# Attention and mixture of experts: the transposed maxima of the next pair one score slot earlier

## Chip, cores and metric

The kernel runs on one core of a Trainium2 chip. The metric is device microseconds from start to end of one execution. Shorter is better. The times below are three executions and one profiled execution of the kernel before.

## What is computed

Attention with rotary embedding, and then a top-1 mixture of experts over its result:

```
q, k, v: (4, 8, 576, 64) fp32                # 4 batches, 8 heads, 576 positions
q_rot, k_rot = rotate(q), rotate(k)
scores = q_rot @ k_rot^T / 8
attn = exp(scores - max(scores)); attn /= sum(attn) + 1e-9
x = (attn @ v) laid out as (2304, 512)       # 2304 tokens
logits = normalized x . normalized expert_emb / tau      # 8 experts
out[token] = gate * (relu(x @ w1[expert]) @ w2[expert])  # 512 -> 1024 -> 512
```

The expert of a token is the argmax of its logits, and its gate is that expert's softmax probability. Most matrix products are made of fp16 or bf16 halves (a high part and a rest), so that the result is close to fp32.

## The kernel before

**Pairs and slots.** The 32 heads are worked on as 16 pairs of heads (0 to 15). A pair has nine score slots: four key tiles of 128 for each head and one tile shared by both (slot 4). In the text, S7 of pair 11 is the score product of slot 7 of that pair (smm, L226 and L230), E7 its exponential on ScalarE (sexp, L241), and M3 of pair 13 the product of slot 3 that is made only to find the row maxima (maxmm, L185). VectorE reduces each of these to a column of the tile m9 (maxred, L191).

**Where the maxima go.** When all nine columns of a pair are there, maxend does two things. Step 0 (L198) transposes m9 on TensorE into a PSUM bank, tile mt. Step 1 copies it on ScalarE as shift minus maximum, in fp16, to the tile mr (L202), and two DMAs of SyncE (L203, L204) put it into row 64 of the tile QB, where the score product of L230 adds it to the scores. So a pair's first L230 needs those DMAs.

**The bank.** mt lies in the PSUM bank with the tag bk0. In turn the same bank holds mt, the first five value products of a pair (pv, group 0; the fp32 ones are L260, the fp16 ones L281 to L283) and, in a few places, tiles of the routing (rank, L503 and L504). Whoever writes it next waits for the last reader: for mt that is VectorE's division of the value products of the pair before (pvend, L298 and L299), or its copy of the rank tile (L509, L510). The first L260 of a pair waits for ScalarE's copy of mt (L202). Score tiles S and M share a ring of three PSUM tiles.

**The order.** Nothing is scheduled by hand on the engines. Each step is entered with a time in units of one score slot, the list is sorted, and the steps are issued in that order; each engine then runs its own instructions in that order and waits by semaphores. Pair i starts at g0 = 9 i. The times come from the table TIMES (L38):

```
mev(f"M{s}", m0 + md * s + cfg.get("mmt", .2), maxmm, i, s)      # m0 = g0 - 14
ev(f"W{s}", g0 + PVL + s + cfg.get("pvt", .3) - .81, pvw, i, s)  # PVL = 7.5; puts the L260 into the score product
me = cfg.get("mend", 12)
mev("Z0", g0 - L + me, maxend, i, 0)                             # L = 14
mev("Z1", g0 - L + me + cfg.get("med", .7), maxend, i, 1)        # med = 0.3
```

For pairs 0 and 1 a table of its own takes the place of mend. In the middle of the kernel three pairs are in work at a time: during the slots of pair 11 TensorE makes the scores of pair 11, the value products of pair 10 and then 11, the maxima products of pair 13, and the transposition of the maxima of pair 12.

**Routing and experts.** Beside the last pairs VectorE computes logits, ranks and lists (finish, early), with one exponential on ScalarE (L516). At the end of early, SyncE loads the number of the most used expert from the tile est (L870), and issues its eight weight loads (L872). ScalarE converts the weights (conv, L694, L695, L698) in between the exponentials of pair 15. Then follow 22 tiles of 128 tokens through two layers.

Of the kernel before, what the change touches and what calls it, by code (L numbers as in the profile page):

```python
# [34 lines left out]
SY = SX * SW * SW  # L35

ORDER = ((0, 0, 0), (1, 0, 0), (0, 0, 1), (1, 0, 1), (0, 1, 0), (1, 1, 0))
TIMES = {"pe1": 1.06, "pvlead": 7.5, "mend": 11.5, "fin": 3, "w": 0.3, "pbufs": 13, "vat": -1, "med": 0.3, "sst": 1.6, "mct": 0.25, "pvt": 0.3, "pe0": 0.9, "d": 0.6, "rdt": 0.9, "e": 0.5, "c0": 135, "fin2": 2.5, "sq": 0.8, "max0": [[-21, 0.5], [-5, 1], [4.5, 0.9]], "start": [-30, -13, -4, 2.6], "le": -3.5, "vet": 1.2, "mmt": 0.2, "mlead": 14, "klo": 1, "me0": [-13.5, 6.6], "mdir": 3, "ve0": -16, "v0": 3, "pl": [[0, 0, 0, 0], [0, 3, 2, 5]], "setup": [-59.5, -25, -20.9, -19.2, -59.4, -14], "l3": -12, "rk": 14, "ls": 52, "dt": 0.6, "t0": 148.5, "ta": 0.25, "wlead": 10, "cut1": 126, "glead": 20, "s": 0.6, "fin3": -0.45, "r01": [[-30.0, -29.1, -28.2, -27.3, -24.6, -26.4, -25.5, -23.7, -22.8, -21.0], [-25, -24.9, -24.8, -15.5, -14, -20.8, -20.7, -20.6, -15, -13.5]], "bw": 0, "cp": [0, 2, 4, 6], "c0d": 1, "lg1": 0.5, "free": [[2.3, 2.3, 1], [3.5, 3.5, 1], [6.2, 6.2, 0]], "fgap": 1.2}  # L38


def attention(tc, ctx0, ctx, ctx2, ins, xs, R, at, bank, cfg):
# [744 lines left out]
def build(tc, ins, out, cfg=None):  # L786
    cfg = {**TIMES, **(cfg or {})}
    nc = tc.nc
# [217 lines left out]
```

## Times and profile before

| | us |
|---|---|
| three executions | 592.35, 588.22, 587.76 |
| median | 588.22 |
| profiled execution, its own time | 585.0 |
| its span | 582.8 |
| TensorE busy (weight loads apart) | 524.2 |
| VectorE busy | 491.9 |
| ScalarE busy | 344.1 |
| GpSimd busy | 252.1 |

Attention takes about the first 330 us of the span, and the experts the rest. A row of the timeline is the start in us, the duration in us, the engine (PE TensorE's products, PEld its weight loads, DVE VectorE, ACT ScalarE, SPq SyncE's queue), the line, the operation, what it writes and reads, the shapes, how many were merged, and in brackets how long the engine was idle before it and what ended that. Ends of matrix products are modelled.

### The profile page before, as it was taken

What the parts mean: (1) busy time and instruction counts of PE and PEld (TensorE: products, weight loads), DVE (VectorE), ACT (ScalarE), POOL (GpSimd) and SP (SyncE); (2) the same over time, 40 slices, a digit from 0 to 9 for tenths busy, and PEclk for the clock granted to TensorE, in tenths of its full rate; (3) what the DMA queues carried; (4) which work ended last, traced back from release to release, by engine and by line L of the source; (5) the groups of instructions that cost most, each with busy time, mean ns of one, the idle gap of its engine ahead of it and who ended that gap; (6) DMA issues with size and microseconds to landing.
All of it is one profiled execution on the core that took longest, in us unless ns stands there. A gap on an engine that the chain in (4) does not pass through costs nothing. (4 is left out here: it accounts for less than half of the span.)

```text
span 582.8 us, 15753 instructions
## 1 busy us (share of the span) xinstructions
PE 524.2 (90%) x6062; PEld 413.6 (71%) x6062; DVE 491.9 (84%) x778; ACT 344.1 (59%) x578; POOL 252.1 (43%) x174
## 2 busy tenths in 40 slices
PE   1599999999998999799887899999999999999993
PEld 0336778877887887678787888778778768768761
DVE  5886898889899889988865575699999999999981
ACT  2133444555544555246347543679989989989962
POOL 7668765556687555710005132213323323323211
PEclk9999999999999999799997989999999999999998
DMA  8577566568465785145126301378995115431100
GB/s 293 140 199 230 147 184 188 143 183 217 127 186 170 210 214 154 31 111 156 50 84 243 121 4 38 94 234 281 311 326 174 49 47 179 134 112 39 57 21 32
DMA packets 42945, 86.11 MB, mean 148 GB/s; under 512 B 8422, under 2 KB 25702, under 8 KB 42864
## 3 DMA queue, kind: packets, MB, share of 16 engines
q1 hardware_dynamic: 39344, 74.46, 42.3%
q0 software_dynamic: 3520, 10.58, 5.7%
q8 instruction: 49, 0.80, 0.6%
q14 instruction: 32, 0.26, 0.2%
HBM read 115.84 MB, written 10.56 MB: 217 GB/s over the span
## 5 line engine op out<-in xcount | busy, mean ns | idle before, releaser
L699 DVE SCALAR_TENSOR_TENSOR w<-raw,w 128x1024 f16<-128x1024 f32 x148 | 177.3, 1239 | 11.4 <-ACT w L698 11.1
L241 ACT ACTIVATE p<-st 128x576 f32<-128x576 f32 x144 | 93.7, 650 | 134.6 <-PE st L230 131.8
L698 ACT ACTIVATE w<-raw 128x1024 f16<-128x1024 f32 x148 | 148.5, 1057 | 0.0
L191 DVE TENSOR_REDUCE m<-mx 128x1 f32<-128x576 f32 x144 | 106.0, 749 | 33.2 <-PE mx L185 21.6
L735 PEld LDWEIGHTS <-w 128*128 128x128 f16 x2112 | 121.3, 99 | 4.7
L735 PE MATMUL h<-xTm,w 128*128 128x128 f16 x2112 | 123.6, 220 | 0.0
L756 PE MATMUL yp<-w,hT 128*128 128x512 f16 x528 | 120.8, 379 | 0.0
L260 PEld LDWEIGHTS pv<-V,p 128*128 128x128 f32 (+1 forms) x640 | 87.4, 188 | 24.3 <-issue 13.8
L761 POOL DMA_INDIRECT out<-y,sidx x22 | 32.8, 1490 | 159.6 <-ACT y L760 159.6
L226 PE MATMUL st<-QAB,KA 128*128 128x288 f16 x320 | 90.0, 302 | 12.5 <-DVE m L191 11.5
L260 PE MATMUL pv<-V,p 128*128 128x73 f32 (+1 forms) x640 | 94.6, 261 | 4.7 <-ACT mr L202 4.7
L250 DVE TENSOR_TENSOR p<-p 128x576 f16<-128x576 f32 x80 | 92.5, 1159 | 0.6 <-ACT p L241 0.6
L756 PEld LDWEIGHTS <-hT 128*128 128x128 f16 x528 | 50.8, 98 | 52.9 <-issue 0.2
L230 PE MATMUL st<-QAB,KB 65*128 65x288 f16 x320 | 70.2, 302 | 0.2 <-DMA QAB<-mr 0.2
L282 PE MATMUL pv<-V,p 128*128 128x72 f16 (+1 forms) x480 | 63.8, 203 | 0.0
L281 PE MATMUL pv<-V,p 128*128 128x73 f16 (+1 forms) x480 | 63.4, 201 | 0.0
L283 PE MATMUL pv<-V,p 128*128 128x73 f16 (+1 forms) x480 | 63.2, 199 | 0.0
L185 PE MATMUL mx<-KA,QAB 128*128 128x288 f16 x260 | 52.1, 290 | 0.8 <-ACT p L241 0.8
L281 PEld LDWEIGHTS <-p 128*128 128x128 bf16 (+1 forms) x480 | 48.7, 106 | 4.4 <-issue 1.4
L282 PEld LDWEIGHTS <-p 128*128 128x128 bf16 (+1 forms) x480 | 47.1, 103 | 2.5
L283 PEld LDWEIGHTS <-p 128*128 128x128 f16 (+1 forms) x480 | 47.9, 105 | 0.0
L149 POOL TENSOR_TENSOR qlo<-q,qhi 128x576 f16<-128x576 f32 x14 | 19.0, 1358 | 64.6 <-ACT qhi L144 64.6
(159 smaller groups left out, 703.7 us busy)
## 6 DMA issues: line engine op xcount, KB each, us to landing
raw<-w SPq DMA_DIRECT2D x152, 512.0 KB
q<-qk SPq DMA_DIRECT2D x16, 576.0 KB
k<-qk SPq DMA_DIRECT2D x16, 576.0 KB
vt<-vt SPq DMA_DIRECT2D x16, 320.0 KB
v<-v SPq DMA_DIRECT2D x16, 320.0 KB
QAB<-qhi SPq DMA_DIRECT2D x32, 144.0 KB
KA<-khi SPq DMA_DIRECT2D x64, 72.0 KB
xs<-x SPq DMA_DIRECT2D x8, 512.0 KB
```

Of the source, the lines that this page charges most:

```text
L191: nc.vector.tensor_reduce(out=st[i]["m9"][:, s:s + 1], in_=st.pop(("mx", i, s))[:, :, :288], op=ALU.max, axis=AX.XY)
L226: nc.tensor.matmul(ps[:, c, :288], lhsT=KA[n][:, cols(s, h)], rhs=QA[n][:, H0[h] + c * 288:H0[h] + c * 288 + 288], start=(h == hs[0]), sto ...
L241: nc.scalar.activation(out=p.rearrange("p (c x) -> p c x", c=2), in_=st.pop(("s", i, s))[:, :, :288], func=AF.Exp, scale=0.125)
L250: nc.vector.tensor_tensor(out=lo, in0=p, in1=hi, op=ALU.subtract)
L260: nc.tensor.matmul(o, lhsT=lt, rhs=rt, start=first, stop=False, skip_group_check=True)
L281: nc.tensor.matmul(o[:, 0:73], lhsT=ph, rhs=vv[:, 0:73], start=False, stop=False, skip_group_check=True)
L282: nc.tensor.matmul(o[:, 1:73], lhsT=ph, rhs=vv[:, 73:145], start=False, stop=False, skip_group_check=True)
L283: nc.tensor.matmul(o[:, 0:73], lhsT=pl, rhs=vv[:, 0:73], start=False, stop=(kk == 4), skip_group_check=True)
L698: nc.scalar.activation(out=d[:, 0], in_=raw[c], func=AF.Copy, scale=SW)
L699: nc.vector.scalar_tensor_tensor(out=d[:, 1], in0=raw[c], scalar=SW, in1=d[:, 0], op0=ALU.mult, op1=ALU.subtract)
L735: nc.tensor.matmul(ps[:, f], lhsT=wd[:, wi, jj * 512 + f * 128:jj * 512 + f * 128 + 128], rhs=xt[:, xi, 2 * jp + jj], start=(jp == 0 and k ...
L756: nc.tensor.matmul(ps, lhsT=ht[:, hi, 2 * c + ii], rhs=wd[:, wi, ii * 512:(ii + 1) * 512], start=(c == 0 and k == 0), stop=(c == 3 and k = ...
```

## The change

One number of the table is changed, mend:

```diff
-TIMES = {"pe1": 1.06, "pvlead": 7.5, "mend": 11.5, "fin": 3, ...
+TIMES = {"pe1": 1.06, "pvlead": 7.5, "mend": 10.5, "fin": 3, ...
```

The transposition of pair i moves from g0 - 2.5 to g0 - 3.5 and the copy from g0 - 2.2 to g0 - 3.2, for pairs 2 to 15. That is from slot 6 of the pair before to its slot 5. The DMAs go with the copy. On SyncE the order stays as it was, and so do VectorE's and GpSimd's orders. Three places show what moves (the number at the end of a name is that of the tile; tiles made later have other numbers where the order changed).

TensorE, in the slots of pair 11, the transposition of the maxima of pair 12 (m_12; mx_1 is M1 of pair 13, pv with p_7 is pair 10's):

```order
 L185 LDWEIGHTS QAB_132
 L185 MATMUL mx_1_3636<-KA_133,QAB_132 128x288
+L198 MATMUL mt_3648<-ident,m_12_3287 9x128
 L281 LDWEIGHTS p_7_3371
 L281 MATMUL pv_3544<-V_0_141,p_7_3371 128x73
```

It now stands behind M1, ahead of nine value products and S6; it stood behind M2, ahead of nine value products and S7.

ScalarE, the same slots: the exponential of the routing (L516) and the exponentials E5, E6, E7 of pair 11 (p_5, p_6, p_7):

```order
 L241 ACTIVATE p_4_3587<-st_4_3576 128x576
 L241 ACTIVATE p_5_3634<-st_5_3627 128x576
+L202 ACTIVATE mr_3660<-mt_3648,shiftt 9x128
 L516 ACTIVATE dd_3487<-dd_3487 128x80
-L241 ACTIVATE p_6_3671<-st_6_3664 128x576
-L202 ACTIVATE mr_3690<-mt_3679,shiftt 9x128
+L241 ACTIVATE p_6_3677<-st_6_3670 128x576
 L241 ACTIVATE p_7_3704<-st_7_3697 128x576
```

The copy stood behind L516 and E6 and now stands ahead of both.

ScalarE, in the slots of pair 14, the copy of the maxima of pair 15, the last one ahead of the weight loads on SyncE:

```order
 L241 ACTIVATE p_5_4550<-st_5_4541 128x576
-L241 ACTIVATE p_6_4571<-st_6_4564 128x576
-L202 ACTIVATE mr_4587<-mt_4576,shiftt 9x128
+L202 ACTIVATE mr_4566<-mt_4552,shiftt 9x128
+L241 ACTIVATE p_6_4577<-st_6_4570 128x576
 L241 ACTIVATE p_7_4611<-st_7_4604 128x576
```

It stood behind E6 and now stands behind E5.

## Rows read from the trace of the kernel before

**Rows 1.** View of the tile mr: who waited for it (us, times).
```profile
  PEld pv L260: 10.4, 15
  PE pv L260: 4.7, 8
```
**Rows 2.** Timeline (columns as said above), maxima of pair 5, old place.
```profile
119.06 0.34 ACT L202 ACTIVATE mr<-mt,shiftt 9x128 f16<-9x128 f32 x1
...
119.36 0.28 PE L226 MATMUL st<-QAB,KA 128*128 128x288 f16 x1 [0.23 <-DVE m L191]
...
119.49 0.41 PE L260 MATMUL pv<-V,p 128*128 128x73 f32 x2
```
**Rows 3.** Timelines of VectorE and TensorE, maxima of pair 5, new place.
```profile
114.59 0.19 DVE L299 TENSOR_TENSOR xe<-pv,pvr 128x40 f32<-128x40 f32 x1
...
116.18 0.20 PE L281 MATMUL pv<-V,p 128*128 128x73 f16 x1
...
117.47 0.28 PE L226 MATMUL st<-QAB,KA 128*128 128x288 f16 x1 [0.81 <-DVE m L191]
```
**Rows 4.** Timeline, maxima of pair 2.
```profile
69.02 0.44 PE L260 MATMUL pv<-V,p 128*128 128x73 f32 x2 [0.20 <-ACT mr L202]
...
70.29 0.76 DVE L191 TENSOR_REDUCE m<-mx 128x1 f32<-128x576 f32 x1 [0.40 <-PE mx L185]
```
**Rows 5.** Timeline, maxima of pair 12, from the new place to S7.
```profile
239.86 0.27 PE L281 MATMUL pv<-V,p 128*128 128x73 f16 x1
...
240.95 0.15 DVE L510 COPY cnt<-rank 128x8 f32<-128x8 f32 x1
...
241.75 1.14 DVE L250 TENSOR_TENSOR p<-p 128x576 f16<-128x576 f32 x1
...
242.52 0.42 PE L198 MATMUL mt<-ident,m 128*9 128x128 f32 x1
243.18 0.28 PE L226 MATMUL st<-QAB,KA 128*128 128x288 f16 x1
```
**Rows 6.** Timeline, maxima of pair 12, S7 of pair 11 and what follows.
```profile
245.35 0.44 PE L260 MATMUL pv<-V,p 128*128 128x73 f32 x2 [1.89 <-ACT mr L202]
...
246.64 0.76 DVE L191 TENSOR_REDUCE m<-mx 128x1 f32<-128x576 f32 x1 [1.26 <-PE mx L185]
```
**Rows 7.** Windows: span, length, busy us of PE, PEld, DVE, ACT, POOL, granted clock, DMA.
```profile
238.00:242.00 4.00, 4.00 (x27) 3.49 (x27) 4.00 (x8) 0.65 (x1) 3.92 (x3) 0.50 0.00 0
246.00:250.00 4.00, 4.00 (x30) 3.43 (x28) 2.87 (x10) 2.60 (x5) 0.00 (x0) 0.57 0.19 42
```
**Rows 8.** Timeline, maxima of pair 13, S7 of pair 12 and what follows.
```profile
263.47 0.28 PE L226 MATMUL st<-QAB,KA 128*128 128x288 f16 x1
...
264.43 0.44 PE L260 MATMUL pv<-V,p 128*128 128x73 f32 x2 [0.68 <-ACT mr L202]
...
265.70 0.76 DVE L191 TENSOR_REDUCE m<-mx 128x1 f32<-128x576 f32 x1 [1.68 <-PE mx L185]
```
**Rows 9.** Timeline, maxima of pair 14, S7 of pair 13 and what follows.
```profile
281.83 0.28 PE L226 MATMUL st<-QAB,KA 128*128 128x288 f16 x1
...
282.97 0.44 PE L260 MATMUL pv<-V,p 128*128 128x73 f32 x2 [0.85 <-ACT mr L202]
...
284.24 0.76 DVE L191 TENSOR_REDUCE m<-mx 128x1 f32<-128x576 f32 x1 [1.22 <-PE mx L185]
```
**Rows 10.** Timelines of ScalarE and VectorE, from the maxima of pair 15 to the weights.
```profile
296.37 0.65 ACT L241 ACTIVATE p<-st 128x576 f32<-128x576 f32 x1 [0.56 <-PE st L230]
...
298.00 0.14 DVE L588 CAST est<-em 1x1 int32<-1x1 f32 x1
...
298.07 0.34 ACT L202 ACTIVATE mr<-mt,shiftt 9x128 f16<-9x128 f32 x1
...
305.31 1.06 ACT L694 ACTIVATE ws<-raw 128x1024 f32<-128x1024 f32 x1 [3.85 <-issue]
```
**Rows 11.** View of line L870, SyncE: duration in ns, first and last start.
```profile
L870 SPq TENSOR_LOAD <-est x1: 802/802/802, 299.9 to 299.9; - x1
```

More of the change, by code (lines that the diff above doesn't have):

```diff
@@ L37 @@
 ORDER = ((0, 0, 0), (1, 0, 0), (0, 0, 1), (1, 0, 1), (0, 1, 0), (1, 1, 0))
-TIMES = {"pe1": 1.06, "pvlead": 7.5, "mend": 11.5, "fin": 3, "w": 0.3, "pbufs": 13, "vat": -1, "med": 0.3, "sst": 1.6, "mct": 0.25, "pvt": 0.3, "pe0": 0.9, "d": 0.6, "rdt": 0.9, "e": 0.5, "c0": 135, "fin2": 2.5, "sq": 0.8, "max0": [[-21, 0.5], [-5, 1], [4.5, 0.9]], "start": [-30, -13, -4, 2.6], "le": -3.5, "vet": 1.2, "mmt": 0.2, "mlead": 14, "klo": 1, "me0": [-13.5, 6.6], "mdir": 3, "ve0": -16, "v0": 3, "pl": [[0, 0, 0, 0], [0, 3, 2, 5]], "setup": [-59.5, -25, -20.9, -19.2, -59.4, -14], "l3": -12, "rk": 14, "ls": 52, "dt": 0.6, "t0": 148.5, "ta": 0.25, "wlead": 10, "cut1": 126, "glead": 20, "s": 0.6, "fin3": -0.45, "r01": [[-30.0, -29.1, -28.2, -27.3, -24.6, -26.4, -25.5, -23.7, -22.8, -21.0], [-25, -24.9, -24.8, -15.5, -14, -20.8, -20.7, -20.6, -15, -13.5]], "bw": 0, "cp": [0, 2, 4, 6], "c0d": 1, "lg1": 0.5, "free": [[2.3, 2.3, 1], [3.5, 3.5, 1], [6.2, 6.2, 0]], "fgap": 1.2}
+TIMES = {"pe1": 1.06, "pvlead": 7.5, "mend": 10.5, "fin": 3, "w": 0.3, "pbufs": 13, "vat": -1, "med": 0.3, "sst": 1.6, "mct": 0.25, "pvt": 0.3, "pe0": 0.9, "d": 0.6, "rdt": 0.9, "e": 0.5, "c0": 135, "fin2": 2.5, "sq": 0.8, "max0": [[-21, 0.5], [-5, 1], [4.5, 0.9]], "start": [-30, -13, -4, 2.6], "le": -3.5, "vet": 1.2, "mmt": 0.2, "mlead": 14, "klo": 1, "me0": [-13.5, 6.6], "mdir": 3, "ve0": -16, "v0": 3, "pl": [[0, 0, 0, 0], [0, 3, 2, 5]], "setup": [-59.5, -25, -20.9, -19.2, -59.4, -14], "l3": -12, "rk": 14, "ls": 52, "dt": 0.6, "t0": 148.5, "ta": 0.25, "wlead": 10, "cut1": 126, "glead": 20, "s": 0.6, "fin3": -0.45, "r01": [[-30.0, -29.1, -28.2, -27.3, -24.6, -26.4, -25.5, -23.7, -22.8, -21.0], [-25, -24.9, -24.8, -15.5, -14, -20.8, -20.7, -20.6, -15, -13.5]], "bw": 0, "cp": [0, 2, 4, 6], "c0d": 1, "lg1": 0.5, "free": [[2.3, 2.3, 1], [3.5, 3.5, 1], [6.2, 6.2, 0]], "fgap": 1.2}
 def attention(tc, ctx0, ctx, ctx2, ins, xs, R, at, bank, cfg):
```

## The prediction

> **What bounds the kernel now.** I first asked who waits for the copy that is moved: the weight loads ahead of L260 wait 10.4 us for it in 15 places, and the products themselves stand idle for 4.7 us in 8 [rows 1]. The reader should see that these two differ: most of the 15 waits cost TensorE nothing, because something else held it at the same moment. So I went through the places in the timeline, one by one, and asked at each what would be late next.
>
> In the even middle of the attention (maxima of pairs 3 to 11) the old place looks like that of pair 5 [rows 2]. S7 begins at 119.36, released by VectorE's reduction, and L260 follows 0.13 us later, as it does where nothing is waited for. The copy ended at 119.40, in time by a hair. VectorE sets the pace there; the wait for the copy runs beside the wait for the reduction.
>
> In the last four places the picture is another. At the maxima of pair 12 TensorE is idle for 1.89 us ahead of L260, and VectorE then stands idle for 1.26 us waiting for the maxima product that comes after it [rows 6]. At pair 13 it is 0.68 us and then 1.68 us of VectorE's [rows 8], at pair 14 0.85 and 1.22 us [rows 9]. There the copy is late because ScalarE does squares, the routing's exponential and E6 first, and TensorE holds up everybody. The chain goes S7, maxima product, reduction. At pair 15 the copy matters through SyncE: it ends at 298.41, its two DMAs are ahead of the load of est in SyncE's order, and that load starts only at 299.9 [rows 11] although est was written at 298.14. The weight loads follow, and ScalarE stands for 3.85 us before its first conversion at 305.31 [rows 10].
>
> **The change part by part.** Nothing is added or removed; 14 transpositions, copies and pairs of DMAs move one slot forward.
>
> *Transposition, pairs 2 to 11.* At the new place of pair 5 TensorE is there at 116.18. The bank was given back at 114.78 (L299), 1.40 us earlier, and S6 waits 0.81 us for VectorE anyway [rows 3]. The transposition lengthens the queue by less than that, so it costs nothing; if that cover were gone, it would cost its own time, which leaves the old place. For pairs 3 to 11 I count 0. Bounds: 0.1 us lost over the nine, and 1.0 us won if ScalarE's squares in two of them hold more than they seem to.
>
> *Maxima of pair 2.* TensorE waits 0.20 us for the copy, and VectorE 0.40 us for TensorE after it [rows 4]. I take 0.3 us, between 0.20 and 0.40.
>
> *Maxima of pair 12.* Here the bank is not free at the new place: the rank tile of the routing lies in it. TensorE is there at 239.86, but VectorE reads the rank tile until 241.10 [rows 5]. So the transposition, and behind it nine value products, S6, M2 and S7, wait until 241.16, if I allow the 0.05 us that lie between a reduction's end and its follower elsewhere (an estimate): a new stall of 1.30 us. The work from 239.86 to the start of S7 at 243.18 is 3.32 us, the transposition included, and 0.13 us more bring L260: 241.16 + 3.32 + 0.13 = 244.61, against 245.35. The copy is done long before, as it no longer stands behind L516 and E6. Gain 0.74 us, and VectorE's idle 1.26 us has room for it.
> The clock adds to it. TensorE was granted half rate (1.2 GHz) at the stall, 0.50 in 238 to 242, and again 0.57 in 246 to 250, after its idle 1.89 us [rows 7]. If the second stretch goes with that idle time, up to 4.0 x (1 - 0.57) = 1.72 us come on top: 2.46 us. If instead half rate lasts through S7, the 1.29 us from L260 to the reduction after it [rows 6] take up to as much again, and the gain is 0.74 - 1.29 = -0.5 us. I take 1.0 us, near the value at unchanged rates; bounds -0.5 and 2.4.
> The Trainium skill (TensorE: Matmul & The Clock Gate, A second HAM failure mode: psum-queue depth-cycling) says that short idles between groups of products, while the engine goes round its PSUM banks, are enough to throw the clock back and forth. That speaks against this change, which puts a wait for a bank in a stretch at half rate; by it the lower bound would hold here and the sum would be 2.7 us. The trace agrees so far that 1.89 us of idle stood ahead of the second stretch.
>
> *Maxima of pair 13.* L260 would follow S7's start by 0.13 us, at 263.60 instead of 264.43: 0.83 us [rows 8]. The transposition's time moves from ahead of S7 to ahead of S6, which cancels. Bounds 0.68 (idle alone) and 0.9.
>
> *Maxima of pair 14.* The same: 281.96 instead of 282.97, 1.01 us [rows 9]. The rank tile of this pair is read earlier, so I count no stall. Bounds 0.85 and 1.2 (VectorE's idle).
>
> *Maxima of pair 15.* The copy stands behind E5 instead of E6, so it can start when E5 ends at 297.02 at the latest, instead of 298.07 [rows 10]. SyncE comes to est 1.05 us earlier, at 298.85, still later than est is written. I take 1.05 us: ScalarE's wait for the weights is the longest of this stretch and TensorE runs dry behind it. Bounds 0, if the weights come no earlier, and 1.2.
>
> No queue is passed that would lose by it: SyncE's order is the same, and of GpSimd nothing moves. VectorE's order is the same too.
>
> Sum: 0 + 0.3 + 1.0 + 0.83 + 1.01 + 1.05 = 4.2 us. The experts start from the lists and the weights that the attention's end and SyncE give them, so they move forward as they are. The profiled execution took 585.0 us (span 582.8 and 2.2 us around it), which gives 580.8. The median of the runs shown is 588.2, 3.2 us above; on that footing I predict **584.0 us**.
>
> **The rivals.**
> *Nothing arrives.* The gains of pairs 12 to 14 fall where VectorE is as full as TensorE (4.00 of 4.00 us in 238 to 242 [rows 7]), and the weights' landing is set by something else. For it: the nine even pairs show that shape. Against it: VectorE's idle times behind each wait. 588.2 us, within half a microsecond.
> *Half rate goes on* through S7 after the new stall, the lower bound of that place: pair 12 gives -0.5 instead of 1.0, 2.7 us in all, 585.5 us. For it: the new stall lies at half rate. Against it: the longer idle goes.
> *More than forecast.* The nine even pairs have room of their own and S7 starts 0.3 us earlier in each: 2.7 us more, 581.3 us. Against it: 119.36 is VectorE's release.
> *Slower: the transposition waits for more of VectorE's queue than it needs.* If its wait counts every instruction issued before it, not just L299, then at pair 5 it waits for the reduction that releases S7 at 119.36 [rows 2]. S6 would come no earlier than 119.3 instead of 117.47, at least 1.8 us in each of nine pairs, some 16 us: 600 us with the gains taken off. It decides from a wait beyond the 1.3 us that S6 leaves. Against it: at pair 12 the old transposition started at 242.52 while a subtraction issued before it ran from 241.75 to 242.89 [rows 5]. That the change does nothing is excluded by the order.
>
> **How the numbers follow.** Forecast 0.60, nothing arrives 0.19, half rate 0.11, more than forecast 0.05, slower 0.05. The forecast's own bounds are the sums of the lower ends, 0.2 - 0.1 - 0.5 + 0.68 + 0.85 + 0 = 1.1 us, and of the upper ends, 0.4 + 1.0 + 2.4 + 0.9 + 1.2 + 1.2 = 7.1 us: 581.1 to 587.1. The range takes in the case of nothing too: **581.0 to 588.4**. One per cent, about what a measurement can tell from no change, is 5.9 us: faster than 582.3 needs the upper quarter of the forecast's bounds or the case of more, 0.15 + 0.05 = 0.20. Slower by over 1% is the slower rival, 0.05. Within 1%: 0.75.
>
> **What the profile after would show.** L260 no longer waits for L202 anywhere from pair 2 on. At the new place of pair 12 the transposition starts 0.06 us after L510, behind some 1.3 us of idle, and at no other pair does TensorE wait there. The reductions after S7 of pairs 12 and 13 lose about 0.8 and 1.0 us of idle. L870 starts some 0.7 us after est is written, instead of 1.8. Between the copy of pair 3 and that of pair 11 the distance stays as it was. Wrong would be a stall at L198 in the even pairs, or an L694 that comes as late as before, relative to E5 of pair 14.

## The result and the profile after

The changed kernel takes **583.8 us** in the median of 14 executions (580.4 to 586.5), the kernel before 589.4 us beside it (14 executions, 584.2 to 593.9). The ratio is 0.9908, with a 95% interval of 0.9879 to 0.9936: 5.4 us less, between 3.8 and 7.1. The profiled execution took 584.7 us, with a span of 582.5 us, all but the 582.8 us of before. The two profiles can therefore be compared place by place, but not by their spans.

The view of the tile mr in the kernel after answers to [rows 1]. What is left is pair 1, which was not moved:

```profile
  PEld pv L260: 0.7, 1
  PE pv L260: 0.2, 1
```

The view of TensorE's waits from 40 to 305 us (engine, line, waited for: us in total, times, longest) shows one wait at the transposition L198, and one alone:

```profile
PE st L226 <- DVE m L191: 12.8, 27, 1.2
PE rank L503 <- DVE xe L299: 2.4, 1, 2.4
PE rank L503 <- DVE ohall L495: 1.5, 1, 1.5
PE mt L198 <- DVE nrm L511: 1.3, 1, 1.3
```

In the even middle the timeline shows the transposition of pair 5 with no wait ahead of it, and S6 released by VectorE's reduction as it was in [rows 3]:

```profile
118.46 0.41 PE L185 MATMUL mx<-KA,QAB 128*128 128x288 f16 x2
118.71 0.27 PE L198 MATMUL mt<-ident,m 128*9 128x128 f32 x1
...
120.00 0.28 PE L226 MATMUL st<-QAB,KA 128*128 128x288 f16 x1 [0.71 <-DVE m L191]
```

At pair 12 the new wait stands in TensorE's timeline, and VectorE's and ScalarE's timelines show what ends it and what follows. They answer to [rows 5, 6]:

```profile
243.44 0.37 PE L198 MATMUL mt<-ident,m 128*9 128x128 f32 x1 [1.34 <-DVE nrm L511]
```
```profile
241.72 1.35 DVE L506 TENSOR_SCALAR nrm<-nrm 128x10 f32<-128x10 f32 x1
242.99 0.23 DVE L509 TENSOR_TENSOR rk<-rank,ohall 128x80 f32<-128x80 f32 x1
243.14 0.15 DVE L510 COPY cnt<-rank 128x8 f32<-128x8 f32 x1
243.22 0.20 DVE L511 RECIPROCAL nrm<-nrm 128x10 f32<-128x10 f32 x1
...
245.12 1.28 DVE L515 TENSOR_TENSOR dd<-dd,nrm 128x80 f32<-128x80 f32 x1
...
251.02 0.17 DVE L527 TENSOR_SCALAR gt<-gt 128x10 f32<-128x10 f32 x1
```
```profile
243.85 0.36 ACT L202 ACTIVATE mr<-mt,shiftt 9x128 f16<-9x128 f32 x1 [1.54 <-PE mt L198]
246.44 0.27 ACT L516 ACTIVATE dd<-dd 128x80 f32<-128x80 f32 x1 [2.23 <-DVE dd L515]
```

The copy is now 2.6 us ahead of the routing's exponential L516, which itself waits for VectorE's L515. VectorE's reduction after S7 waits 0.11 us where it waited 1.26 [rows 6], but the reduction behind it waits 1.41 us where it waited 0.39. At pair 13 VectorE's reduction after S7 waits 0.64 us where it waited 1.68 [rows 8]. At pair 15 the load of est starts at 299.5, 0.6 us after est is written, and the first conversion waits 3.44 us, not 3.85 [rows 10, 11]. VectorE's timeline, ScalarE's, and the view of L870:

```profile
265.99 0.76 DVE L191 TENSOR_REDUCE m<-mx 128x1 f32<-128x576 f32 x1 [0.64 <-PE mx L185]
```
```profile
297.15 0.65 ACT L241 ACTIVATE p<-st 128x576 f32<-128x576 f32 x1 [0.56 <-PE st L230]
297.70 0.34 ACT L202 ACTIVATE mr<-mt,shiftt 9x128 f16<-9x128 f32 x1
...
304.92 1.06 ACT L694 ACTIVATE ws<-raw 128x1024 f32<-128x1024 f32 x1 [3.44 <-issue]
```
```profile
L870 SPq TENSOR_LOAD <-est x1: 802/802/802, 299.5 to 299.5; - x1
```

**Why the spans are alike.** The first three rows are TensorE's timeline after, in the slots of pair 1; the rest are windows of the same trace (span, length, busy us of PE, PEld, DVE, ACT, POOL, granted clock, DMA). The last three answer to [rows 7].

```profile
63.45 0.44 PE L226 MATMUL st<-QAB,KA 128*128 128x288 f16 x1
...
68.64 0.28 PE L226 MATMUL st<-QAB,KA 128*128 128x288 f16 x1
68.76 0.34 PE L260 MATMUL pv<-V,p 128*128 128x73 f32 x2
```
```profile
60.00:65.00 5.00, 5.00 (x47) 3.65 (x47) 3.35 (x8) 1.47 (x3) 3.45 (x3) 1.00 0.15 34
238.00:242.00 4.00, 3.25 (x39) 2.63 (x38) 3.97 (x7) 0.34 (x1) 3.92 (x3) 0.65 0.10 21
246.00:250.00 4.00, 4.00 (x36) 3.50 (x35) 2.41 (x7) 2.12 (x5) 0.30 (x1) 0.57 0.00 0
280.00:284.00 4.00, 4.00 (x36) 3.41 (x35) 2.13 (x5) 1.85 (x4) 0.00 (x0) 0.57 0.06 10
```

The score product of 288 columns lasts 0.44 us up to 66.9 us and 0.28 us from 68.64 on: half rate (1.2 GHz) and full rate (2.4 GHz). In the trace before it lasts 0.28 to 0.30 us from 62.6 us on. That is 6 us more at half rate. E5 of pair 1 starts at 69.68 us, 3.0 us later than in the trace before, just ahead of the first moved transposition at 69.72; at E0 of pair 2 it is 2.5 us. The window view doesn't tell this, for it gives 1.00: the trace has no clock record ahead of 68.56 us (62.12 in before), and a stretch without a record is shown as 1.00. A further half-rate stretch of 3.4 us stands near 280 us, where before had none. So the profile of after lost about 2.5 us by E0 of pair 2 and some at 280, and won them back in the last pairs.

### The profile page after: what moved, and what is told of

It reads as the page before. It is cut to its first block, busy times and chain, and to the rows that moved or that the text cites. A ratio compares the mean times of both kernels' runs of the same rounds, so it can differ in the third digit from the quotient of the medians.

```text
span 582.5 us, 15755 instructions
## 1 busy us (share of the span) xinstructions
PE 526.4 (90%) x6062; PEld 416.1 (71%) x6062; DVE 491.4 (84%) x778; ACT 344.4 (59%) x578; POOL 248.7 (43%) x174
## 5 line engine op out<-in xcount | busy, mean ns | idle before, releaser
L241 ACT ACTIVATE p<-st 128x576 f32<-128x576 f32 x144 | 93.5, 650 | 136.4 <-PE st L230 132.7
L226 PE MATMUL st<-QAB,KA 128*128 128x288 f16 x320 | 91.2, 306 | 13.7 <-DVE m L191 12.8
L260 PEld LDWEIGHTS pv<-V,p 128*128 128x128 f32 (+1 forms) x640 | 89.2, 191 | 18.9 <-issue 14.3
L260 PE MATMUL pv<-V,p 128*128 128x73 f32 (+1 forms) x640 | 94.7, 261 | 0.2 <-ACT mr L202 0.2
L250 DVE TENSOR_TENSOR p<-p 128x576 f16<-128x576 f32 x80 | 91.4, 1147 | 0.5 <-ACT p L241 0.5
L230 PE MATMUL st<-QAB,KB 65*128 65x288 f16 x320 | 71.3, 306 | 0.0
L281 PE MATMUL pv<-V,p 128*128 128x73 f16 (+1 forms) x480 | 64.4, 203 | 0.0
L283 PE MATMUL pv<-V,p 128*128 128x73 f16 (+1 forms) x480 | 64.1, 201 | 0.0
```

Source lines behind the costliest of these rows:

```text
L226: nc.tensor.matmul(ps[:, c, :288], lhsT=KA[n][:, cols(s, h)], rhs=QA[n][:, H0[h] + c * 288:H0[h] + c * 288 + 288], start=(h == hs[0]), sto ...
L241: nc.scalar.activation(out=p.rearrange("p (c x) -> p c x", c=2), in_=st.pop(("s", i, s))[:, :, :288], func=AF.Exp, scale=0.125)
L250: nc.vector.tensor_tensor(out=lo, in0=p, in1=hi, op=ALU.subtract)
L260: nc.tensor.matmul(o, lhsT=lt, rhs=rt, start=first, stop=False, skip_group_check=True)
L281: nc.tensor.matmul(o[:, 0:73], lhsT=ph, rhs=vv[:, 0:73], start=False, stop=False, skip_group_check=True)
L283: nc.tensor.matmul(o[:, 0:73], lhsT=pl, rhs=vv[:, 0:73], start=False, stop=(kk == 4), skip_group_check=True)
```

## The experiments

The profiled executions are compared by distances that do not depend on the start: from the first exponential of a pair (E0, L241) to that of the next. The number behind the stroke is the time at half rate within the distance, from the trace's clock records. The transposition of pair 12 stands in the slots of pair 11, and so on. Distances of the runs below, worked out from the starts of the 144 exponentials:

| us / us at half rate | pair 12 (E0 of 11 to 12) | pair 13 (12 to 13) | pair 14 (13 to 14) | pair 15 (E0 of 14 to E4 of 15) |
|---|---|---|---|---|
| before | 24.55 / 10.2 | 17.77 / 0 | 18.54 / 0 | 27.68 / 6.8 |
| after | 23.60 / 10.2 | 16.82 / 0 | 19.04 / 3.4 | 26.50 / 6.8 |
| change again | 23.58 / 10.2 | 16.82 / 0 | 19.05 / 3.4 | 26.31 / 6.8 |
| pairs 2 to 11 moved | 23.22 / 3.4 | 17.76 / 0 | 19.50 / 3.4 | 28.16 / 6.8 |
| pairs 12 to 14 moved | 22.57 / 3.4 | 16.82 / 0 | 19.05 / 3.4 | 28.39 / 6.8 |
| pair 15 moved | 26.09 / 10.3 | 19.03 / 3.3 | 18.55 / 0 | 27.49 / 6.8 |
| pair 12 moved | 23.63 / 10.2 | 17.76 / 0 | 19.50 / 3.4 | 28.02 / 6.8 |
| L516 later, nothing moved | 21.90 / 6.8 | 17.76 / 0 | 19.31 / 3.4 | 28.45 / 6.8 |
| two slots for pairs 12 to 15 | 21.98 / 6.8 | 16.82 / 0 | 17.32 / 0 | 25.03 / 3.4 |

Where half rate takes as long and the edit at that place is the same, the distances of pairs 12 to 14 repeat within 0.2 us, with one exception: the old place of pair 12 (24.55 and 26.09). Times below are ratios to executions of the kernel before on the same chip, and what they make of its 588.0 to 588.4 us.

**The parts.** Each moves a part of the 14 pairs (one line of each edit, put together).

```diff
-        me = cfg.get("mend", 12)
+        me = 10.5 if 2 <= i <= 11 else 11.5      # e1_mid
+        me = 10.5 if 12 <= i <= 14 else 11.5     # e2_late
+        me = 10.5 if i == 15 else 11.5           # e3_last
+        me = 10.5 if i == 12 else 11.5           # e9_only12
```

> Only the maxima of pairs 2 to 11 move; those of pairs 12 to 15 stay in the old place. Theory A (the prediction's account: the copy sits on the path only at pairs 2 and 12 to 15): 0.3 us less than before, from pair 2, and the distance between the copies of pair 3 and pair 11 as before. Rival B (the change gave 5.4 us where 4.2 were counted, and the rest comes from the ten even pairs): 1.2 to 2.7 us less. Rival C (the gain is mostly TensorE's clock: an earlier transposition ends the half rate at the start of the attention sooner, which in the two traces ended at 62 and at 68 us): 2 to 4 us less in the median, and a narrower spread than before's 584 to 594.

Measured: 1.0011 (0.9985 to 1.0037), +0.6 us (-0.9 to +2.2). From E0 of pair 3 to E0 of pair 11 it takes 135.73 us; in the runs that left these pairs alone it is 135.77, 135.77 and 135.88, and 136.12 in before. (Four other traces have 136.5 to 137.4 there, three with these pairs moved and one without; in each, one L230 waited 0.6 to 1.5 us for the DMAs of mr.) At pair 2 the step from E6 to E7 of pair 1 falls from 1.97 to 1.40 us, and the step from E5 to E6, where the transposition now stands, grows from 1.40 to 1.50: 0.47 us less from E5 to E7. It is still there at E0 of pair 2 in this trace and in after (7.35 and 7.34 us from E5, 7.81 in before); in change again E0 came 0.4 us later and it was gone (7.83). B and C fall: the ten pairs give next to nothing, and the half rate of the start ends where it ends (the spread is 584 to 592, as before's).

> Only the maxima of pairs 12, 13 and 14 move. Theory A: 2.8 us less than before (1.0 at pair 12, 0.83 at pair 13, 1.01 at pair 14); TensorE waits 1.3 us at the transposition of pair 12, behind VectorE's read of the rank tile, and no longer for the copy at these three. Rival B: no more than that, since its surplus lies in the even pairs, 2.8 too. Rival C: 0 to 1.5 us, the rest being the clock in the early pairs.

Measured: 0.9937 (0.9906 to 0.9968), -3.7 us (-5.5 to -1.9). A holds in the time and in the waits for the copy, of which none is left at these three. The new stall is not the 1.3 us that was expected but twice as long. TensorE's timeline:

```profile
242.55 0.27 PE L198 MATMUL mt<-ident,m 128*9 128x128 f32 x1 [2.58 <-DVE nrm L511]
```

In this stretch TensorE was at half rate only from 243.7 us on, after the stall. With as much half rate, 3.4 us, the place takes 22.57 us here and 23.22 in e1_mid, which has the old place.

> Only the maxima of pair 15 move. Theory A: 1.05 us less than before: SyncE comes to the load of est (L870) right after est is written, the weights land earlier and the first conversion (L694) with them. Rival D (the landing of the weights is set by something else, or the experts do not start from it): 0, with L870 earlier and L694 where it was, relative to the exponentials of pair 15.

Measured: 0.9977 (0.9945 to 1.0010), -1.4 us (-3.2 to +0.6), by itself unclear. The traces decide for A in what the weights do: from E5 of pair 14 to the first conversion L694 it is 7.77 us here and 7.77 in after, against 8.94 in before. In the five traces with pair 15 moved by one slot it is 7.39 to 7.77 us, in the five with its old place 8.53 to 8.94; to E0 of pair 15 it is 9.43 to 9.81 against 10.57 to 10.98. Further on it is not clear: from E5 of pair 14 to E4 of pair 15 this run takes 19.50 us, hardly less than the 19.69 to 20.46 of the old place, where the whole change takes 18.32 and 18.51.

> Only the maxima of pair 12 move, by one slot. Theory A (the first account, with the size corrected: the copy was held for 1.9 to 3.2 us in the traces of the old place, the new stall is 1.3 us): 1.0 to 2.0 us less than before. The account on record before the result counted 1.0. Rival G (half rate goes on through the new stall and takes it back): 0.5 us more than before to 0.3 less.

Measured: 0.9961 (0.9937 to 0.9986), -2.3 us (-3.7 to -0.8). G falls. TensorE waits 1.53 us at L198, and half rate lasts from 238.4 to 248.7, right through the stall and S7; the place still takes 23.63 us against 24.55 and 26.09 with as much half rate in the old place.

The three disjoint parts add up to 0.6 - 3.7 - 1.4 = -4.5 us, within the interval of the whole (3.8 to 7.1 us less).

**What held the copy of pair 12.** The transposition stays in its old place, and only the exponential of the routing is issued two steps later (shortened; it is moved for the first 10 tiles alone, the conditions are left out):

```diff
-        nc.scalar.activation(out=dd, in_=dd, func=AF.Exp)
         yield
         v.tensor_copy(pi, ri)
         yield
+        nc.scalar.activation(out=dd, in_=dd, func=AF.Exp)   # for the first 10 tiles
```

> The kernel before, transpositions in the old place, and one thing moved: the routing's exponential (L516) stands behind E6 and the copy of pair 12 instead of ahead of both. Theory A (at pair 12 it was the copy's place in ScalarE's queue that cost, not the transposition's in TensorE's): the wait of 1.9 to 3.2 us at L260 of that place falls under 1 us, and 1.0 to 2.5 us come off before without moving any transposition. Rival E (VectorE's work there, 1.3 us each for L506, L515 and the subtractions, sets the pace): within 0.5 us of before, with VectorE's idle time gone as well.

Measured: 0.9952 (0.9923 to 0.9981), -2.8 us (-4.5 to -1.1). ScalarE's timeline (L522 is the exponential in its new place) and TensorE's waits from 40 to 305 us:

```profile
243.78 0.65 ACT L241 ACTIVATE p<-st 128x576 f32<-128x576 f32 x1 [2.02 <-PE st L230]
244.47 0.36 ACT L202 ACTIVATE mr<-mt,shiftt 9x128 f16<-9x128 f32 x1
245.74 0.27 ACT L522 ACTIVATE dd<-dd 128x80 f32<-128x80 f32 x1 [0.91 <-DVE dd L515]
```
```profile
PE pv L260 <- ACT mr L202: 2.0, 6, 0.7
```

The longest wait at L260 falls from 1.9 us [rows 6] to 0.7, which is pair 13's, and none is left at pair 12. The place takes 21.90 us with 6.8 us at half rate, where e1_mid, with only 3.4, takes 23.22, and no transposition was moved. E falls. What cost at pair 12 was that the copy stood behind an exponential whose input VectorE delivers late.

The traces with the old place say how late. In e1_mid the rows of the stall are TensorE's and ScalarE's:

```profile
244.19 0.44 PE L260 MATMUL pv<-V,p 128*128 128x73 f32 x2 [3.16 <-ACT mr L202]
```
```profile
238.35 0.65 ACT L241 ACTIVATE p<-st 128x576 f32<-128x576 f32 x1 [4.88 <-PE st L230]
243.09 0.27 ACT L516 ACTIVATE dd<-dd 128x80 f32<-128x80 f32 x1 [4.09 <-DVE dd L515]
```

L516 starts 4.74 us after E5 there, 4.60 in e3_last and 4.63 in before. VectorE sets that, whatever TensorE's rate. In before TensorE was at half rate on the way to L260 and so stood for only 1.89 us; here it came at full rate and stood for 3.16.

**The new stall.** The whole change, with the transposition of pair 12 behind the nine value products, its copy right after it, and L516 one step later (the lines of L516 are left out):

```diff
-        mev("Z0", g0 - L + me, maxend, i, 0)
-        mev("Z1", g0 - L + me + cfg.get("med", .7), maxend, i, 1)
+        mev("Z0", g0 - L + me + (.31 if i == 12 else 0), maxend, i, 0)
+        mev("Z1", g0 - L + me + (.32 if i == 12 else cfg.get("med", .7)), maxend, i, 1)
```

> The whole change, and at the maxima of pair 12 two things more: the transposition stands behind the nine value products, just ahead of S6, so that the rank tile is read before TensorE gets there; and the routing's exponential (L516) stands behind E6 instead of ahead of the copy and E6. Theory A: the new stall of 1.34 us falls to 0.6 or less and ScalarE's 2.2 us of idle ahead of L516 and E6 go: 0.7 to 1.5 us less than the change, about 6.5 us less than before. Rival E (VectorE is the bound there and takes up whatever TensorE gets): within 0.3 us of the change, 5.4 us less than before.

Measured: 0.9879 (0.9842 to 0.9917), -7.1 us (-9.3 to -4.9). The stall was 0.63 us, about as expected. A second comparison put the change beside it:

> The change once more, as it is, beside the next ones on one chip. Theory A (4.2 us counted, and more where the routing's exponential held the copy of pair 12 longer than in the one trace of before): 4 to 5.5 us less than before. Where its half-rate stretches lie will differ from the trace before; the distance from E0 of pair 12 to E0 of pair 13 should be 16.82 us again where no half rate falls into it, and 17.76 in before.

> The whole change with the transposition of pair 12 behind the nine value products and L516 behind E6, once more, beside the change on one chip. Theory A: 0.6 us less than the change from the shorter stall (0.63 against 1.34 us in the traces), up to 1.5 with ScalarE's idle time. Rival E: the same as the change within 0.3 us.

Measured: the change 0.9933 (0.9907 to 0.9960), -3.9 us (-5.5 to -2.4), so the first result comes again within its interval; the version with the moved transposition 0.9913 (0.9885 to 0.9941), -5.1 us. The intervals overlap, and in this trace the stall was 1.9 us and not 0.63. In both the place takes less (22.98 / 10.2 and 22.51 / 6.8), but the time of the whole does not tell A from E here: inconclusive.

**More lead.** The same change with another number, and with two numbers:

```diff
+TIMES = {... "mend": 9.5, ...                   # e7_two_slots
+        me = 9.5 if i >= 12 else 10.5           # e10_late_two
+TIMES = {... "mend": 8.5, ...                   # e11_three_slots
```

> The change with mend 9.5 instead of 10.5: the maxima stand two slots further forward than before. Theory A (once the copy is in time, more lead buys nothing; the bank is given back 0 to 0.2 us after TensorE gets to the transposition in pairs 3 to 11, and S6 has 0.8 us to cover it): within 1 us of the change in pairs 2 to 11 and 13 to 15. Rival F (the bank is not back yet, and TensorE loses 0.3 us or more at each of nine pairs): 3 us or more slower than the change, with a wait at L198 in every pair.

Measured: 0.9881 (0.9844 to 0.9918), -7.0 us (-9.2 to -4.8). The median, 580.2, is 3.4 us under that of the change beside it. A failed, and F too: pairs 3 to 11 take 135.64 us and TensorE waits at L198 twice. So the next run asked where it was.

> Pairs 2 to 11 at mend 10.5 as in the change, pairs 12 to 15 at 9.5. Theory H (what two slots gained over one lies in the last pairs, where TensorE's idle time and with it the half-rate stretches go, and the lists and est come earlier): as with 9.5 everywhere, 2.5 to 4 us less than the change, some 8 us less than before. Rival I (it lies in pairs 2 to 11): as the change, 5 us less than before.

Measured: 578.7 us, 0.9838 (0.9808 to 0.9869), -9.5 us (-11.3 to -7.7). H holds and I falls: it is the last four pairs. This version has the lowest median of the study. TensorE's waits, 40 to 305 us, and windows of its trace and of the change's (e5_change):

```profile
PE mt L198 <- DVE xe L299: 2.6, 2, 2.4
PE list L552 <- DVE V L129: 1.8, 1, 1.8
PE list L552 <- DVE B L547: 1.1, 1, 1.1
```
```profile
275.00:300.00 25.00, 23.81 (x332) 21.56 (x332) 20.91 (x70) 11.13 (x22) 0.00 (x0) 1.00 0.24 75
```
```profile
275.00:300.00 25.00, 23.28 (x292) 20.32 (x290) 20.86 (x77) 10.65 (x22) 0.00 (x0) 0.93 0.17 49
```

At pair 12 the transposition now stands ahead of the rank tile in the same bank and waits 2.4 us for the division L299, where the rank products waited 2.4 us for it before. In pairs 14 and 15 the table shows 17.32 and 25.03 us, with 3.4 us at half rate where the change has 10.2. Est is written 1.1 us after E5 of pair 14 starts, 1.6 in the change. How much of it is the rate and how much the waits was not taken apart.

> mend 8.5: three slots further forward than before. Theory A (at this place VectorE has not yet divided the value products of the pair before, so the bank is not free): TensorE waits at L198 in nearly every pair, longer than the 0.8 us that it has to spare ahead of the next score product, and the kernel is slower than with 9.5 by 0.5 us or more in each of nine pairs, 5 us or more. Rival J (the products behind the transposition have as much slack as it waits): within 1 us of 9.5.

Measured: 1.0045 (1.0012 to 1.0077), +2.6 us (+0.7 to +4.5). Its trace is of an execution of 597.7 us, above the median of 592.9, so no distance between exponentials is taken from it. TensorE's waits:

```profile
PE mt L198 <- DVE xe L299: 23.1, 11, 4.4
```

A holds: the bank is not back, in nearly every pair. This is not the mechanism of the prediction's slower rival, which had the transposition wait for more of VectorE's queue than it needs. Here it waits for the bank's last reader alone: in each of the 11 waits L198 starts 0.15 us after L299 ends, and VectorE's next instruction, L250, ends 0.6 us or more after L198 has started.

Both at once:

```diff
 # e6_exp_later's edit, and "mend": 9.5
```

> mend 9.5 and the routing's exponential L516 behind E6 instead of ahead of it. Theory A (each takes another wait away: ScalarE's 3.1 us of idle ahead of L516 and E6 goes too): 0.5 to 1.5 us less than with 9.5 alone, some 9 us less than before. Rival E (VectorE sets the pace of that stretch): the same as with 9.5 alone within 0.4 us.

Measured: 0.9860 (0.9826 to 0.9893), -8.2 us (-10.2 to -6.3). It is not told apart from 9.5 alone (-7.0), so it does not decide between A and E, and its median is above e10_late_two's: once the copy stands ahead of L516 anyway, the exponential's place gives nothing that these runs could measure.

## Why the prediction was right

- **Pairs 3 to 11, counted at 0:** right. No wait at L198, and the distance of pair 3 to 11 is that of the kernels that leave them alone.
- **Pair 2, counted at 0.3:** 0.47 us from E5 to E7 of pair 1, a little over the bound of 0.4, and in one of the two traces of the change nothing was left of it at E0 of pair 2. The term was mis-sized there. That TensorE's 0.20 and VectorE's 0.40 us [rows 4] add up, less the 0.10 of the transposition, would fit, but was not tested.
- **Pair 12, counted at 1.0 of -0.5 to 2.4:** 2.3 us (0.8 to 3.7) by itself, an interval that holds the 1.0. Pairs of traces with as much half rate give 0.65 us (3.4 at half rate), 0.95 and 2.46 (10.2). The cause is the one that was foreseen, and two edits that have nothing else in common, e9_only12 and e6_exp_later, take the wait away. The new stall was 1.34 us against 1.30 foreseen, but that agreement is luck: in the other traces of the same edit it was 1.30, 1.53 and 2.58 us. TensorE started 0.15 us after L510, whose end is 243.29, not 0.06. (The profile names L511, which ends at 243.42; the same 0.15 us that lie between L299 and L198 in e11_three_slots, where the next instruction is not waited for, speak for L510 as the one that was waited for.) What was missing in the size is that the old stall, too, ended at a time that VectorE set, 4.6 to 4.7 us after E5, whatever TensorE's rate. The trace of before has the smallest of the three old stalls, 1.89 us against 3.16 and 3.16.
- **Half rate at pair 12:** the rival on the Trainium skill's rule (TensorE: Matmul & The Clock Gate, A second HAM failure mode: psum-queue depth-cycling) had it that half rate goes on through the stall and takes the gain. In the trace half rate did go on, from 239.2 to 249.5 in one stretch where before had two, as this rival had it; but the time at half rate was the same 10.2 us, and the place was shorter by 0.95 us. Nor does half rate go with the stall: e2_late has the longest new stall, 2.58 us, and 3.4 us at half rate there. The prediction's own thought, that the second stretch goes with the idle time at L260, is not borne out either: after 3.16 us of idle e3_last went to half rate at 246.3 us, and e1_mid, after as much, not before 276.8. What sets these stretches stays open.
- **Pair 13, counted at 0.83:** 0.95 us (17.77 to 16.82), the same in every run that moves it by one slot or two and has no half rate there.
- **Pair 14, counted at 1.01:** 0.27 to 0.46 us with 3.4 us at half rate on both sides (19.31 and 19.50 to 19.04), so the term was too large for that case. It was read from a trace without half rate in this pair, where L260 waited 0.85 us; in the traces of the old place with half rate it waited 0.19 us or less. Without half rate the move was not seen with one slot.
- **Pair 15, counted at 1.05:** 1.17 us from E5 to L694 (0.76 to 1.55 over all the traces), by L870 as foreseen. How much of it reaches the experts' start was not told apart.
- **The rivals:** nothing arrives is excluded by the interval. More than forecast is excluded as put, since the even pairs gave nothing. Slower did not come: outside pair 12 no transposition waited at one slot.

The sum of 4.2 us lies in the interval of both comparisons of the change (3.8 to 7.1 and 2.4 to 5.5). That 584.0 came within 0.2 us of the measured 583.8 is luck: the kernel before ran at 589.4 and not 588.2, and the change gave 5.4 and not 4.2. The terms erred both ways too, pair 14's too large and pair 2's too small. The sum was taken off the median and not off the profiled execution's 585.0, and that mattered: 585.0 was at the fast end of before's 584 to 594.

## What to carry to other kernels

Read an in-order queue for who stands ahead of the late instruction and what *that* waits for; moving either of the two takes the wait away (here the copy, or the exponential ahead of it). Before moving work forward into a shared bank, find when its last reader is done: up to two slots of lead were free here or better, and at the third TensorE waited 23 us. How long a stall is depends on when the waiting engine arrives as much as on the engine that ends it, so take its end from the other engine, and not its length from one trace. Where a rate changes between runs, compare distances within the trace rather than spans.

## What the runs showed of the hardware

**A slow start that the window view does not show.** In the windows from 60 to 65 us the view gives a granted clock of 1.00, but products of 288 columns last 0.40 to 0.45 us (1.2 GHz) from 25 us on, where later they last 0.28 (2.4 GHz). The traces have no clock record before the first rise, and the view counts such a stretch as 1.00. The first record, of full rate, stands at 62.1 us in the profile of before and at 68.6 in that of after. From E0 of pair 0 to E0 of pair 2 it takes 41.8 to 44.3 us in the five traces in which nothing of that stretch was moved, and a kernel's own times spread over 8 us.

**VectorE held by GpSimd.** L506 works on 128x10 elements and lasts 1.35 us, L527 on as many 0.17 us. L506 ends at 243.07, and L515 (1.28 us) at 246.40. GpSimd's timeline after:

```profile
241.24 1.81 POOL L141 TENSOR_TENSOR q<-q 128x576 f32<-128x576 f32 x1
243.01 1.40 POOL L137 TENSOR_TENSOR k<-k,cost 128x576 f32<-128x576 f32 x1
244.38 1.93 POOL L139 TENSOR_TENSOR k<-k,sint 128x576 f32<-128x576 f32 x1
```

L141 ends at 243.05 and L139 at 246.31, each less than 0.1 us before the long VectorE instruction does. In 13 of the 14 traces L515 runs beside L139 and lasts 1.28 to 1.31 us. In that of e11_three_slots no GpSimd instruction runs beside it, and the same instruction takes 0.24 us:

```profile
255.24 0.24 DVE L515 TENSOR_TENSOR dd<-dd,nrm 128x80 f32<-128x80 f32 x1
```

The Trainium skill (SBUF — State Buffer, Who interferes with whom) says that the two engines share a pair of ports under an exclusive lock and that, in the cases it lists, the one that issued first holds them for its whole instruction while the other blocks; these rows agree, with L141 and L139 the earlier ones. No run took GpSimd's work away, so how much of the wait of pair 12 began there is not shown; L515 alone is 1.0 us longer.

**Idle time and half rate in the even pairs.** The trace of the three-slot version has half-rate stretches that no other trace has, at 120.2, 137.3 and 157.8 us, each 3.4 us long. TensorE waited 1.87 us at L198 nine times between 84 and 227 us. Waits that ended at 118.63 and 156.42 us came 1.6 and 1.4 us ahead of such a stretch, and one, ended at 137.40, ran when it began. The other six, ended at 84.34, 101.48, 175.18, 192.54, 209.68 and 226.83, were followed by none. So the same wait came with a fall of the clock and without one, and what decides it stays open.
